# A mixture of experts in blocks of 128: rows turned between a block's two products, and blocks without tokens branched over

## The chip, the cores and the metric

The kernel runs on one core of a Trainium2 chip. A core has five engines with queues of their own: TensorE (PE in the profile; its weight loads are listed as PEld), VectorE (DVE), ScalarE (ACT), GpSimd (POOL) and SyncE (SP). They run beside each other and wait for each other by semaphores; transfers are done by DMA engines that SP, ACT and POOL ask. The metric is the device time of one execution in microseconds, and of several runs the median.

## The reference

Two layers. Attention between tokens and a state gives, for each of 8 batches, 512 token rows and 32 state rows of 512 values. Then each row goes to one of 8 experts:

```
logits = np.einsum('bsd,de->bse', x, w_gate)
local_gate = 1.0 / (1.0 + np.exp(-np.einsum('bsd,de->bse', x, w_local).squeeze(-1)))
...
        fresh_e = int(np.argmax(logits[b, s]))
        if s == 0 or local_gate[b, s] < 0.5:
            e = fresh_e
        else:
            e = prev_e if prev_e >= 0 else fresh_e
...
        h = np.maximum(x[b, s] @ w1[e], 0.0)
        out[b, s] = p[e] * (h @ w2[e])
```

w1 of an expert is 512 x 1024 and w2 is 1024 x 512, all in float32. There are 8 x 544 = 4352 rows. Which expert a row gets is known only while the kernel runs. With the inputs that the reference sets up, its own arithmetic gives the eight experts 1568, 600, 544, 512, 544, 40, 0 and 544 rows. In blocks of 128 that is 13, 5, 5, 4, 5, 1, 0 and 5, or 38 blocks.

## The kernel before, in words

`attention` goes through the batches and writes a row per token to DRAM (`rows`): 512 values and 8 gate probabilities. `Routing.route` then finds each token's expert and gives the tokens slots sorted by expert, an expert's slots filled up to whole blocks of 128. However the tokens fall, 34 full blocks and 7 broken ones are enough, so there are always NBLK = 41 blocks; the kernel does all 41, whether or not a block holds a token. `route` leaves three tables in SBUF: `gidx` (which row a slot gathers; row 0 where the slot is empty), `sidx` (where its result goes; a place past the end where it is empty, which the scatter leaves out) and `bei` (the expert of each block).

`experts` does the blocks one after the other. Block k:

- `load(k)`: SP reads the block's expert from `bei` into a register and asks for the two weights, `a` (w1) and `c` (w2), 2 MB each. There are two buffers of each, so `a` of block k + 2 is asked for when the first product of block k is done, and `c` of block k + 2 when its second is done.
- `gather(k)`: POOL asks for the block's 128 rows (`xg`, three buffers).
- DVE picks each row's probability for the block's expert (`own`, `p`).
- PE transposes the 128 x 512 rows in four pieces into PSUM (L428), and DVE copies the result to `x_t` (L430).
- First product (L437): 32 calls, two PE instructions each, from `x_t` and `a`; ACT takes each half out of PSUM with a ReLU into `h` (L439).
- Second product (L442): 8 calls, two instructions each, from `h` and `c`.
- DVE multiplies by the probability (`y`, L444), and POOL scatters the rows to their places (L445).

The program is traced in this order; a scheduler then lays out each engine's queue and puts in the semaphores. Each engine takes its queue strictly in order. On PE the queue reads, block after block: transposes, first product, second product. The first product needs the copy that DVE makes of the transposes just ahead of it.

Of the kernel before, what the change touches and what calls it, by code (L numbers as in the profile page):

```python
# [8 lines left out]
F32 = mybir.dt.float32  # L9
# [8 lines left out]
P = 128  # L18
# [20 lines left out]
def kernel(  # L39
# [33 lines left out]
    bei = keep.tile([1, NBLK], I32, name="bei")  # L73
    wg = keep.tile([P, KT, E + 1], F32, name="wg")
    nc.sync.dma_start(out=wg, in_=wgl.rearrange("p (k e) -> p k e", k=KT))
    # Logits of token (column i of 128, batch b); the last column holds the 32 state tokens.
# [7 lines left out]
    route.route(lt, mx, gidx, sidx, ohb, bei)  # L84
    with ExitStack() as phase:
        experts(phase, tc, bank, w1, w2, ident, rows, gidx, sidx, ohb, bei, out)


def attention(ctx, tc, bank, xn, xt, st, stt, ident, wg, lt, mx, rows):
# [8 lines left out]
    # State, and its transpose, with the heads of a group on the diagonal of blocks.  # L98
# [16 lines left out]
    # The state's gate logits: those of a token are the same mean of them as its values.  # L115
# [24 lines left out]
        # Tokens over state: scores of tokens over (head, state).  # L140
# [28 lines left out]
    def turned(e1, e2):  # L169
        """Both transposed: (head, state) over tokens, and tokens over (head, state)."""  # L170
# [12 lines left out]
    def read(b, a_t, e_t, x_n):  # L183
        # What the state reads, transposed, for pairs of heads; only a head's own block counts.
# [51 lines left out]
    # A batch's softmaxes run beside the products of the batch before it.  # L236
# [11 lines left out]
class Routing:  # L248
    """Tokens' experts, and the tokens of the slots."""
# [31 lines left out]
    def route(self, lt, mx, gidx, sidx, ohb, bei):  # L281
# [3 lines left out]
        # A token's own choice, the first of the largest logits, as 1..8, or 0 where it takes the one before.  # L285
# [14 lines left out]
        # In the order of a batch's tokens: the last choice made.  # L300
# [20 lines left out]
        # A token's place among those of its expert.  # L321
# [15 lines left out]
        nc.vector.tensor_tensor_scan(end[:, 0], ones[:, :E], nblk, 0.0, Alu.mult, Alu.add)  # L337
        first = rt.tile([P, E, 1], F32, name="first")
# [24 lines left out]
        # The experts of the blocks.  # L363
# [12 lines left out]
        # The tokens (from 1; 0 for none) of the slots, by (place in block, block).  # L376
# [16 lines left out]
def experts(ctx, tc, bank, w1, w2, ident, rows, gidx, sidx, ohb, bei, out):  # L393
# [3 lines left out]
    hp = ctx.enter_context(tc.tile_pool(name="hp", bufs=2))  # L397

    def gather(k):
        xg = gp.tile([P, XW], F32, name="xg")  # L400
        nc.gpsimd.indirect_dma_start(out=xg, out_offset=None, in_=rows[:, :],  # L401
                                     in_offset=bass.IndirectOffsetOnAxis(ap=gidx[:, k:k + 1], axis=0))
        return xg

    def load(k):
        e = nc.values_load(bei[0:1, k:k + 1], engines=[ET.SP], min_val=0, max_val=E - 1,
                           skip_runtime_bounds_check_because="the index of an expert")
        a = wp.tile([P, KT, F], F32, name="a")
        nc.sync.dma_start(out=a.rearrange("p k f -> p (k f)"),
                          in_=w1[bass.ds(e, 1)].rearrange("o p x -> (o p) x"))  # L410
        c = wp.tile([P, FK, D], F32, name="c")
# [65 lines left out]
```

## Time and profile before

| | us |
|---|---|
| median of 3 runs (lowest to highest) | 876.18 (876.18 to 879.81) |
| span of the profiled execution | 877.5 |
| first product of block 0 starts | 222.60 |
| y of block 40 starts | 867.91 |
| PE busy | 795.2 |

The page gives no time of the profiled execution beside its span, which is 1.3 us above the median of the runs. Up to about 200 us the core does attention and then finds the experts; the rest is the 41 blocks. In rows of the timeline stand the start, the duration, the engine, the line and operation, out<-in, the count, and in brackets how long the engine stood still before it and who ended that. Matmuls are pipelined, so a group's duration includes the last one's way through the array, and the next group starts before it ends. "L428" is a line of the kernel printed above.

### The profile page before, as it was taken

The page shows a single profiled execution, that of the slowest core. Times are in us where ns is not written, and L with a number is a line of the kernel's source. Part 1 is how long each engine was busy: PE and PEld are TensorE (multiplying, and loading weights), DVE is VectorE, ACT ScalarE, POOL GpSimd, SP SyncE. Part 2 cuts the span into 40 slices and gives each one's busy share as a digit, 9 for nine tenths or more (in the row PEclk, how much of TensorE's full clock was granted, in tenths as well). Part 3 has the DMA queues.
Part 4 walks back from the last instruction along what each step waited for, and adds up shares of the span by engine and source line. Part 5 has one row for each costly group of instructions (what it writes and reads, how often), then busy time and mean ns, then how long its engine had stood idle before and what let it go on. Part 6 is the DMA issues. An engine that isn't in the chain of part 4 may idle for free.

```text
span 877.5 us, 11051 instructions
## 1 busy us (share of the span) xinstructions
PE 795.2 (91%) x4658; PEld 600.2 (68%) x4658; DVE 182.8 (21%) x525; ACT 111.1 (13%) x200; POOL 103.5 (12%) x110
## 2 busy tenths in 40 slices
PE   6899999937899999999999999999999999999995
PEld 6588888927676666766757667576676766767663
DVE  2465555465100101001010010100101001001010
ACT  0333343310000010000100001000010000100000
POOL 2001110000110101101011010110100101001000
PEclk9799999965899999999999999999999999999998
DMA  8145531228488878888788788887888877788730
GB/s 335 49 148 177 198 118 55 102 87 354 155 318 301 297 286 304 321 297 300 277 306 317 292 296 292 307 316 281 297 298 303 316 287 290 292 307 308 271 144 1
DMA packets 25761, 219.41 MB, mean 250 GB/s; under 512 B 3760, under 2 KB 3760, under 8 KB 13168
## 3 DMA queue, kind: packets, MB, share of 16 engines
q1 hardware_dynamic: 14400, 189.29, 58.6%
q0 software_dynamic: 6560, 19.84, 6.0%
q10 hardware_dynamic: 4752, 9.58, 3.0%
q8 instruction: 37, 0.61, 0.3%
q14 instruction: 12, 0.10, 0.0%
HBM read 200.73 MB, written 19.80 MB: 251 GB/s over the span
## 4 chain that ended last, share of the span: by engine, by line
issue 65%; PE 21%; POOL 6%; DMA 4%; DVE 3%; POOLq 0%; SPq 0%; DVEq 0%
POOL out_dram L445 4%; PE ps L138 4%; PE ps L201 3%; PE ps L144 3%; PE ps L188 3%; DMA out_dram<-y,sidx 3%; PE ps L386 2%; POOL xg L401 2%; PE ps L121 2%; PE ps L204 1%; PE ps L178 1%; PE ps L173 1%; DMA sttc<-in_stt_dram 1%; DMA xg<-rows,gidx 0%; PE ps L214 0%
## 5 line engine op out<-in xcount | busy, mean ns | idle before, releaser
L437 PE MATMUL ps<-x_t,a 128*128 128x128 f32 x2624 | 305.9, 278 | 41.0 <-DVE x_t L430 41.0
L437 PEld LDWEIGHTS ps<-x_t,a 128*128 128x128 f32 x2624 | 298.1, 193 | 50.9 <-DVE x_t L430 50.9
L442 PE MATMUL ps<-c,h 128*128 128x512 f32 x656 | 288.3, 592 | 0.0
L442 PEld LDWEIGHTS ps<-c,h 128*128 128x128 f32 x656 | 121.5, 190 | 137.3 <-issue 137.3
L439 ACT ACTIVATE h<-ps 128x512 f32<-128x512 f32 x82 | 49.0, 597 | 632.5 <-PE ps L437 632.5
L401 POOL DMA_INDIRECT xg<-rows,gidx x41 | 40.0, 975 | 553.9 <-PE ps L428 500.0
L444 DVE TENSOR_SCALAR y<-ps,p 128x512 f32<-128x512 f32 x41 | 30.8, 751 | 284.6 <-PE ps L442 284.6
L423 DVE TENSOR_TENSOR own<-xg,ohb 128x8 f32<-128x8 f32 x41 | 6.9, 167 | 300.8 <-DMA xg<-rows,gidx 300.8
L445 POOL DMA_INDIRECT out_dram<-y,sidx x41 | 41.6, 1015 | 69.3 <-DVE y L444 58.0
L144 PEld LDWEIGHTS ps<-std,x_t 128*128 128x128 f32 x256 | 32.2, 197 | 8.8 <-issue 8.8
L428 PEld LDWEIGHTS ps<-ident,xg 128*128 128x128 f32 x164 | 20.7, 143 | 25.5 <-issue 25.5
L201 PE MATMUL ps<-sd,a 128*128 128x256 f32 x128 | 35.3, 398 | 0.0
L138 PE MATMUL ps<-x_t,std 128*128 128x512 f32 x64 | 33.7, 653 | 0.0
L166 POOL TENSOR_TENSOR e<-e,z 128x512 f32<-128x512 f32 x16 | 16.7, 1047 | 142.6 <-DVE z L160 109.6
L144 PE MATMUL ps<-std,x_t 128*128 128x128 f32 x256 | 32.0, 279 | 0.0
L188 PE MATMUL ps<-e,x_n 128*128 128x64 f32 x256 | 29.5, 273 | 0.0
L188 PEld LDWEIGHTS ps<-e,x_n 128*128 128x128 f32 x256 | 29.2, 192 | 0.0
L428 PE MATMUL ps<-ident,xg 128*128 128x128 f32 x164 | 25.1, 276 | 4.3 <-DMA xg<-rows,gidx 4.3
L430 DVE COPY x_t<-ps 128x512 f32<-128x512 f32 x41 | 27.9, 682 | 0.9 <-PE ps L428 0.9
L386 PE MATMUL ps<-bc,pc 128*128 128x41 f32 x80 | 17.3, 415 | 9.9 <-DVE bc L381 9.9
L386 PEld LDWEIGHTS ps<-bc,pc 128*128 128x128 f32 x80 | 17.1, 332 | 10.8 <-issue 10.8
L207 ACT COPY xr<-ps 128x512 f32<-128x512 f32 x32 | 18.8, 586 | 36.6 <-PE ps L201 36.6
(124 smaller groups left out, 343.1 us busy)
## 6 DMA issues: line engine op xcount, KB each, us to landing
a<-in_w_dram SPq DMA_DIRECT2D x41, 2048.0 KB, 7.8
c<-in_w_dram SPq DMA_DIRECT2D x41, 2048.0 KB, 8.9
rows<-xr ACTq DMA_DIRECT2D x8, 1040.0 KB, 4.3
x_t<-in_xt_dram SPq DMA_DIRECT2D x8, 1024.0 KB, 4.8
x_n<-in_xn_dram SPq DMA_DIRECT2D x8, 1024.0 KB, 5.4
xg<-rows,gidx POOLq DMA_INDIRECT x41, 8.4
out_dram<-y,sidx POOLq DMA_INDIRECT x41, 7.6
rows<-xs ACTq DMA_DIRECT2D x8, 65.0 KB, 4.0
```

Of the source, the lines that this page charges most:

```text
L138: nc.tensor.matmul(s2, lhsT=std[:, b, k, :], rhs=x_t[:, k, :], start=(k == 2 * g), stop=(k == 2 * g + 1))
L144: nc.tensor.matmul(s1[:, c * P:c * P + P], lhsT=x_t[:, k, c * P:c * P + P], rhs=std[:, b, k, :], start=(k == 2 * g), stop=(k == 2 * g + 1))
L188: nc.tensor.matmul(rps[:, k, :], lhsT=x_n[:, c, 2 * k:2 * k + 2, :].rearrange("p h d -> p (h d)"), rhs=e_t[k // 2][:, c, 64 * (k % 2):64 * ...
L201: nc.tensor.matmul(v[:, g * GD:g * GD + GD], lhsT=a_t[g][:, c * P:c * P + P], rhs=sd[:, b, g, :], start=True, stop=True)
L386: nc.tensor.matmul(who, lhsT=pc, rhs=bc[:, c], start=(c == 0), stop=(c == COLS - 1))
L401: nc.gpsimd.indirect_dma_start(out=xg, out_offset=None, in_=rows[:, :], in_offset=bass.IndirectOffsetOnAxis(ap=gidx[:, k:k + 1], axis=0))
L428: nc.tensor.transpose(tps[:, j * P:j * P + P], xg[:, j * P:j * P + P], ident)
L437: nc.tensor.matmul(hps[:, i * P:i * P + P], lhsT=a[:, j, m * P:m * P + P], rhs=x_t[:, j, :], start=(j == 0), stop=(j == KT - 1))
L439: nc.scalar.activation(h[:, half * 4:half * 4 + 4, :].rearrange("p m t -> p (m t)"), hps, Act.Relu)
L442: nc.tensor.matmul(yps, lhsT=h[:, m, :], rhs=c[:, m, :], start=(m == 0), stop=(m == FK - 1))
L444: nc.vector.tensor_scalar(y, yps, p, None, Alu.mult)
L445: nc.gpsimd.indirect_dma_start(out=out, out_offset=bass.IndirectOffsetOnAxis(ap=sidx[:, k:k + 1], axis=0), in_=y, in_offset=None, bounds_c ...
```

## The change

The transposes, the copy to `x_t` and the probabilities of block k become a function `turn(k)`. It is called once ahead of the first block, and then within block k for block k + 1, between the two products, together with the loads of block k + 1's weights. The buffers of `experts` are now tiles by hand, numbered by k modulo 2, and modulo 4 for `xg`, so gathers are asked for one block further ahead. `route` writes the number of blocks with tokens to `nbi`, one more small cast on DVE. Every engine reads `nbi` into a register. Blocks 0 to 33 are done always; blocks 34 to 40 stand each within an `If` of the one before, and where the number of blocks is reached, all that is left is jumped over. What is skipped would have written nothing, as such a block's slots are all empty. Comments are dropped as well.

```diff
+        nc.vector.tensor_copy(nbi, end[0:1, 0, E - 1:E])
...
-    wp = ctx.enter_context(tc.tile_pool(name="wp", bufs=2))
-    gp = ctx.enter_context(tc.tile_pool(name="gp", bufs=3))
+
+    fx = ctx.enter_context(tc.tile_pool(name="fx", bufs=1))
     hp = ctx.enter_context(tc.tile_pool(name="hp", bufs=2))
+    as_ = [fx.tile([P, KT, F], F32, name=f"a{i}") for i in range(2)]
+    cs_ = [fx.tile([P, FK, D], F32, name=f"c{i}") for i in range(2)]
+    xgs_ = [fx.tile([P, XW], F32, name=f"xg{i}") for i in range(4)]
+    xts_ = [fx.tile([P, KT, P], F32, name=f"x_t{i}") for i in range(2)]
...
-    xgs = {k: gather(k) for k in range(2)}
-    for k in range(NBLK):
-        a, c = load(k)
-        if k + 2 < NBLK:
-            xgs[k + 2] = gather(k + 2)
-        xg = xgs.pop(k)
-        own = gp.tile([P, E], F32, name="own")
-        nc.vector.tensor_tensor(own, xg[:, D:], ohb[:, k], op=Alu.mult)
-        p = gp.tile([P, 1], F32, name="p")
-        nc.vector.tensor_reduce(p, own, axis=AX, op=Alu.add)
+    def turn(k, xg):
+
         tps = bank()
         for j in range(KT):
             nc.tensor.transpose(tps[:, j * P:j * P + P], xg[:, j * P:j * P + P], ident)
-        x_t = hp.tile([P, KT, P], F32, name="x_t")
+        x_t, own, p = xts_[k % 2], owns_[k % 2], ps_[k % 2]
         nc.vector.tensor_copy(x_t.rearrange("p k t -> p (k t)"), tps)
+        nc.vector.tensor_tensor(own, xg[:, D:], ohb[:, k], op=Alu.mult)
+        nc.vector.tensor_reduce(p, own, axis=AX, op=Alu.add)
+        return x_t, p
+
+    xgs = {k: gather(k) for k in range(3)}
+    ws = {0: load(0)}
+    ready = {0: turn(0, xgs.pop(0))}
+
+    def block(k):
+        a, c = ws.pop(k)
+        x_t, p = ready.pop(k)
         h = hp.tile([P, FK, P], F32, name="h")
...
+        if k + 1 < NBLK:
+            ws[k + 1] = load(k + 1)
+            ready[k + 1] = turn(k + 1, xgs.pop(k + 1))
+        if k + 3 < NBLK:
+            xgs[k + 3] = gather(k + 3)
         yps = bank()
...
+    n = nc.values_load(nbi[0:1, 0:1], min_val=NJ, max_val=NBLK,
+                       skip_runtime_bounds_check_because="a number of blocks")
+    for k in range(NJ):
+        block(k)
+    with ExitStack() as held:
+        for k in range(NJ, NBLK):
+            held.enter_context(tc.If(n > k))
+            block(k)
```

What this makes of the queues is shown at three places. A wait in brackets names what the instruction waits for: DMAHW the weights, DMASW a gather or scatter, else an engine. First PE, one block in the middle of the stage, before (L428 transposes, L437 first product, L442 second product):

```order
L428 MATMUL ps<-ident,xg 128x128 [waits DMASW2_49,PE_49]
L428 MATMUL ps<-ident,xg 128x128 x3
L437 MATMUL ps<-x_t,a 128x128 [waits DMAHW1_49,DVE_49]
L437 MATMUL ps<-x_t,a 128x128 x15
L437 MATMUL ps<-x_t,a 128x128 [waits PE_49]
L442 MATMUL ps<-c,h 128x512 [waits DMAHW2_49,Activation_49]
L442 MATMUL ps<-c,h 128x512 x3
L442 MATMUL ps<-c,h 128x512 [waits Activation_49]
```

and the same block now (L447 first product, L427 transposes, L458 second product):

```order
L447 MATMUL ps<-x_t_1736,a_1728 128x128 [waits DMAHW1_49,DVE_49]
L447 MATMUL ps<-x_t_1736,a_1728 128x128 x15
L447 MATMUL ps<-x_t_1736,a_1728 128x128 [waits PE_49]
L427 MATMUL ps<-ident,xg_1731 128x128 [waits DMASW3_49,PE_49]
L427 MATMUL ps<-ident,xg_1731 128x128 x3
L458 MATMUL ps<-c_1730,h 128x512 [waits DMAHW2_49,Activation_49]
L458 MATMUL ps<-c_1730,h 128x512 x3
L458 MATMUL ps<-c_1730,h 128x512 [waits Activation_49]
```

The transposes, now the next block's, have moved from ahead of the first product to between the two; the first product's wait for DVE is for a copy that has the whole second product ahead of it in PE's queue.

Then DVE, the same part of the stage, before (L430 the copy to x_t, L444 y, L423 and L425 the probabilities):

```order
L430 COPY x_t<-ps 128x512 [waits PE_49]
L425 TENSOR_REDUCE p<-own 128x1 [waits DVE_49]
L423 TENSOR_TENSOR own<-xg,ohb 128x8 [waits DMASW0_49]
L444 TENSOR_SCALAR y<-ps,p 128x512 [waits DMASW7_49,PE_49]
L430 COPY x_t<-ps 128x512 [waits PE_49]
```

and now (L429 the copy, L460 y, L430 and L431 the probabilities):

```order
L431 TENSOR_REDUCE p_1739<-own_1737 128x1 [waits DVE_49]
L430 TENSOR_TENSOR own_1737<-xg_1733,ohb 128x8 [waits DMASW7_49,DVE_49]
L429 COPY x_t_1735<-ps 128x512 [waits PE_49]
L460 TENSOR_SCALAR y<-ps,p_1740 128x512 [waits DMASW0_49,PE_49]
L431 TENSOR_REDUCE p_1740<-own_1738 128x1 [waits DVE_49]
```

The copy, which came behind the y of the block before, now comes ahead of it, and it has `own` ahead of it, which waits for a gather.

Last PE where block 33 ends and block 34 begins; before, the queue goes on there as in the first piece:

```order
L458 MATMUL ps<-c_1730,h 128x512 [waits Activation_49]
L458 MATMUL ps<-c_1730,h 128x512 x3
L465 TENSOR_LOAD nbi [waits DVE_49]
L469 COMPARE_AND_BRANCH
L447 MATMUL ps<-x_t_1735,a_1727 128x128 [waits DMAHW7_49,DVE_49,PE_49]
L447 MATMUL ps<-x_t_1735,a_1727 128x128 x15
```

The number of blocks is read into a register here, not earlier, and a comparison with a branch stands ahead of the block; one such branch stands ahead of each of the blocks 35 to 40 too, and the other four engines have the same rows in their queues.

More of the change, by code (lines that the diff above doesn't have):

```diff
@@ L83 @@
         attention(phase, tc, bank, xn, xt, st, stt, ident, wg, lt, mx, rows)
-    route.route(lt, mx, gidx, sidx, ohb, bei)
+    route.route(lt, mx, gidx, sidx, ohb, bei, nbi)
     with ExitStack() as phase:
-        experts(phase, tc, bank, w1, w2, ident, rows, gidx, sidx, ohb, bei, out)
+        experts(phase, tc, bank, w1, w2, ident, rows, gidx, sidx, ohb, bei, nbi, out)
 def attention(ctx, tc, bank, xn, xt, st, stt, ident, wg, lt, mx, rows):
@@ L279, in __init__, with route @@
         self.consts = iof, tok1, far, before, ones, ev, down, full, on
-    def route(self, lt, mx, gidx, sidx, ohb, bei):
+    def route(self, lt, mx, gidx, sidx, ohb, bei, nbi):
         nc, rt, bank, ident = self.nc, self.rt, self.bank, self.ident
```

10 lines of the change are left out of this document (6 added, 4 removed).

## The prediction

> **What bounds the kernel now.** I read three views in this order: the page's busy times and chain, the list of waits, then the timeline of one block. Names: P1 is a block's first product, P2 its second, T the four transposes of a block's rows, the copy is the move of T's result from PSUM to x_t, y is the scaled result.
>
> ```profile
> PE 795.2 (91%) x4658; PEld 600.2 (68%) x4658; DVE 182.8 (21%) x525; ACT 111.1 (13%) x200; POOL 103.5 (12%) x110
> issue 65%; PE 21%; POOL 6%; DMA 4%; DVE 3%; POOLq 0%; SPq 0%; DVEq 0%
> PE ps L437 <- DVE x_t L430: 41.0, 41, 1.0
> ```
>
> PE is the busy engine. The chain of waits puts 65% on "issue", that is, it cannot follow the expert stage and tells nothing there. The last row does: PE's wait in a block is for the copy, 1.0 us each time, 41 times.
>
> ```profile
> core 0: us, PE busy (x) PEld busy (x) DVE busy (x) ACT busy (x) POOL busy (x), PEclk, DMA share, GB/s
> 50.00:186.00 136.00, 130.55 (x950) 113.19 (x949) 73.20 (x238) 49.66 (x98) 13.61 (x13) 0.99 0.38 135
> 222.00:227.00 5.00, 4.40 (x20) 4.40 (x21) 1.28 (x6) 0.00 (x0) 0.94 (x1) 0.50 0.30 94
> 271.84:743.60 471.76, 441.60 (x2521) 318.21 (x2521) 47.53 (x121) 35.83 (x60) 59.79 (x61) 1.00 0.82 300
> 806.00:822.00 16.00, 14.72 (x84) 10.60 (x84) 1.86 (x5) 1.19 (x2) 1.91 (x3) 1.00 0.86 304
> 838.00:854.00 16.00, 14.99 (x87) 10.88 (x88) 1.35 (x2) 1.19 (x2) 1.26 (x2) 1.00 0.29 118
> 854.00:870.00 16.00, 13.87 (x79) 9.69 (x77) 0.75 (x1) 1.20 (x2) 1.18 (x2) 1.00 0.01 1
> ```
>
> The row of 30 blocks has PE busy 441.6 of 471.76 us at clock 1.00, and the DMA engines at 0.82. The last two rows tell two things. The weights have stopped by then (share 0.29, then 0.01), and, as the times below show, blocks 39 and 40 are no shorter for it: DMA is not what paces a block. And 854 to 870 moves 1 GB/s, some 16 KB, where a scatter of 128 full rows is 262 KB: block 39's scatter writes nothing, which fits the count of 38 blocks with tokens out of the reference's choices. Blocks 38, 39 and 40 compute for nobody.
>
> Here is block 1 to block 2, and the end:
>
> ```profile
> 240.40 7.41 PE L437 MATMUL ps<-x_t,a 128*128 128x128 f32 x64 [1.00 <-DVE x_t L430]
> 247.65 7.03 PE L442 MATMUL ps<-c,h 128*128 128x512 f32 x16
> 254.51 0.60 PE L428 MATMUL ps<-ident,xg 128*128 128x128 f32 x4
> 255.38 0.68 DVE L430 COPY x_t<-ps 128x512 f32<-128x512 f32 x1
> 256.12 7.41 PE L437 MATMUL ps<-x_t,a 128*128 128x128 f32 x64 [1.01 <-DVE x_t L430]
> ...
> 853.59 7.41 PE L437 MATMUL ps<-x_t,a 128*128 128x128 f32 x64 [1.01 <-DVE x_t L430]
> 860.84 7.03 PE L442 MATMUL ps<-c,h 128*128 128x512 f32 x16
> 867.91 0.75 DVE L444 TENSOR_SCALAR y<-ps,p 128x512 f32<-128x512 f32 x1 [14.37 <-PE ps L442]
> 868.94 0.98 POOL L445 DMA_INDIRECT out_dram<-y,sidx  x1 [14.74 <-DVE y L444]
> ```
>
> Starts count, since ends overlap. P1 takes 7.25 us of the block (240.40 to 247.65), P2 6.86 (to 254.51), T with the wait 1.61 (to 256.12): a block is 15.72, and (853.59 - 240.40) / 39 = 15.723 says that all 39 are so.
>
> **The change part by part.**
>
> *T moved between P1 and P2.* The wait goes only if P2 covers the copy. T ends, the copy follows 0.27 us later and takes 0.68, so x_t is there about 1 us into P2's 6.86. On DVE the copy of block k+1 now has own of block k+3 ahead of it, which waits for a gather; those rows are asked for after the scatter of block k-3, about two blocks earlier, and land within 10.6 us at the worst:
>
> ```profile
> a<-in_w_dram SPq DMA_DIRECT2D x41, 2048.0 KB, 7.8
> c<-in_w_dram SPq DMA_DIRECT2D x41, 2048.0 KB, 8.9
> DMA to landing us min/median/max: 3.6/8.4/10.6
> ```
>
> (the last row is the gather's). P2 does not wait longer for the second half of h than now: T only comes between. What T, P1 and P2 cost when nothing stops PE is read from pitches:
>
> ```profile
> 241.28 5.97 PE L437 MATMUL ps<-x_t,a 128*128 128x128 f32 x52
> 57.25 0.66 PE L173 MATMUL ps<-ident,e 128*128 128x128 f32 x4
> 57.75 0.60 PE L178 MATMUL ps<-ident,e 128*128 128x128 f32 x4
> 58.18 0.60 PE L173 MATMUL ps<-ident,e 128*128 128x128 f32 x4
> ```
>
> 52 instructions of P1 last 5.97 us; less the last one's own 0.274 that is 5.70 / 51 = 0.1117 each, 64 of them 7.15. The 0.10 up to 7.25 is the restart after the wait. Four transposes in an unbroken row take 0.43 (57.75 to 58.18) to 0.50 (57.25 to 57.75). So the new block is 7.15 + 6.86 + 0.47 = 14.48. Bounds: 7.15 + 6.86 + 0.43 = 14.44 below, and 7.25 + 6.86 + 0.60 = 14.71 above, if P1 keeps its restart and T counts with its whole record. I take 14.48, since attention shows such changes of shape without a gap.
>
> *The first block.* PE runs it half at clock 0.50 (row 222 to 227 above); that stays.
>
> ```profile
> 222.60 9.48 PE L437 MATMUL ps<-x_t,a 128*128 128x128 f32 x64 [0.78 <-DVE x_t L430]
> 231.92 7.03 PE L442 MATMUL ps<-c,h 128*128 128x512 f32 x16
> ```
>
> P2 of block 0 starts at 231.92; with T ahead of it, block 1 starts at 231.92 + 0.47 + 6.86 = 239.25 instead of 240.40.
>
> *Three blocks fewer.* Blocks 1 to 37 are 37 x 14.48 = 535.8, so P2 of block 37 ends at 775.0 and its y starts 0.2 later (y of block 40 starts 0.21 after 853.59 + 7.25 + 6.86 = 867.70): 775.2 instead of 867.9, 92.7 less. Of that the three blocks are 3 x 15.72 = 47.2 and the rest, 45.5, is the wait with the restart. Block 37 still loads weights and turns rows for block 38; both lie in the 14.48 and the free DMA time.
>
> *What the branches add.* The page has no branch and no register load as rows. Nearest is SP, which reads a block's expert into a register between two issues, and the cast that is added sits beside a scan of eight values:
>
> ```profile
> 190.54 0.17 DVE L337 TENSOR_TENSOR_SCAN end<-ones,nblk 128x8 f32<-128x8 f32 x1
> 194.36 0.34 SPq L412 DMA_DIRECT2D c<-in_w_dram  x1
> 195.21 0.33 SPq L409 DMA_DIRECT2D a<-in_w_dram  x1
> ```
>
> 195.21 - 194.70 = 0.51 for the load and what the address needs. PE has one register load and four branches into blocks 34 to 37. Lower bound 0: PE's sequencer may do them while P2's last matmuls, 0.43 each, are still running. Upper bound 5 x 0.51 = 2.6, if each stops PE for as long as SP needed. I take 1.0, nearer the lower end, since the load's own wait is for a value written 600 us earlier. [...] The cast adds 0.17 to DVE's row of work before the gathers. SP, ACT, DVE and POOL branch too. Behind them queue the next weights, h, the copy and the gathers, each wanted several us later or, for the weights, 14 us: a is asked for when P1 of block k ends, lands after 7.8 and is used 0.47 + 6.86 + 14.48 = 21.8 later.
>
> *The end.* From y's start to the span's end are 877.5 - 867.9 = 9.6 us.
>
> ```profile
> L473 POOLq DRAIN  x3: 40/107/7987, 868.7 to 877.2; - x3
> L473 PEldq DRAIN  x2: 13/3112/6212, 861.7 to 877.0; - x2
> L473 SPq DRAIN  x3: 7/7/7, 871.3 to 877.0; - x3
> ```
>
> POOL's drain of 7.99 us fills nearly all of it; SP had its last landing by 871.3. The last scatter now writes 32 rows instead of none, and lands, by the gather's 3.6 with little else running, at most 1.5 later than 871.3: hidden beside the drain. Each engine's one jump over blocks 38 to 40 comes at the end too. [...]
>
> The sum: -92.7 + 0.17 + 1.0 + 0.5 = -91.0, so the span goes from 877.5 to 786.5. The profiled execution stands 1.3 above the median of the runs, 876.18; against the median it is **785**. Own range: 14.44 a block and no costs give 782; 14.71 (+8.5), branches at 2.6 (+1.6) and a bare jump (+3.1) give 798. So 781 to 798.
>
> **The rivals.**
>
> *Entering a block costs a fetch.* If the branch into a block, and not only the jump past them, makes an engine ask memory for its instructions, PE stands still at each. Price by the shortest round trip here, 3.6: four entries and the last jump are 18, less the 1.5 counted: 785 + 16.5 = 801. For it speaks that nothing in this trace excludes it; against it, the blocks follow each other in the order of the program, so that nothing new is asked for. [...]
>
> *The weights become the bound.* A block moves 4.19 MB of weights and 0.53 of rows; 0.82 x 15.72 = 12.9 us of DMA time. If 0.86, the highest share of a block here, is all that can be had, a block is 12.9 / 0.86 = 15.0 and the time 785 + 37 x 0.52 = 804. Against it: each load waits for its buffer, and each block has stretches without any transfer, as this half microsecond (PE, clock, DMA share, GB/s):
>
> ```profile
> 248.00:248.50 0.50, 0.50 (x2) 1.00 0.00 0
> ```
>
> *The change does not do what it says.* Either no block is skipped (three more at 14.48: 828) or PE waits elsewhere for 1.24 a block (37 x 1.24 = 46: 831). The order of instructions and the row 854 to 870 speak against both.
>
> *Slower.* One mechanism: PE is now busy without a pause and its granted clock falls for the whole stage. Below 535.8 / (535.8 + 91) = 0.855 the kernel is slower than before; at 0.80 it would be 785 + 134 = 919. For it: the clock does move here (0.50 in the row 222 to 227). Against it: that was after idleness, and 130.55 of 136 us busy in attention kept 0.99.
>
> **How the numbers follow.** Forecast 0.77; fetch at each entry 0.11; weights 0.07; change without one of its effects 0.03; slower 0.02. What the two likeliest rivals would give is 801 and 804, and some of each lies below, so the range is 779 to 803. A measurement here can't tell 0.5%, about 4 us, from no change; all but the slower case lie far past it: faster 0.97, same 0.01, slower 0.02.
>
> **What would show it.** Right: P1 starts 14.4 to 14.6 apart from block 1 to 33; no PE wait for the copy; the gap before P1 of blocks 34 to 37 under 1 us; 38 pairs of products; from y of block 37 to the end about 10 us. Wrong: a gap of 3 to 4 us before each of those four blocks (fetch); PE waiting for a or c (weights); a clock under 1.00 after 240 us; an end well over 13 us, which would be the jump.

## The result, and the profile after

| | us |
|---|---|
| median before, beside these runs (4 runs) | 877.4 (876.18 to 879.81) |
| median of the changed kernel (4 runs) | 784.18 (783.41 to 785.57) |
| ratio, 95% interval | 0.893, 0.891 to 0.895 |
| span of the profiled execution, and its time | 783.0, and 784.79 |
| span predicted, and time predicted | 786.5, and 785 |

The kernel is 93.2 us faster, 0.8 us from the forecast. The same three views, of the changed kernel: the page's busy times and chain, the wait list (PE's row, which now stands for one wait instead of 41) and the window of the middle of the stage.

```profile
PE 739.7 (94%) x4410; PEld 568.0 (73%) x4410; DVE 185.4 (24%) x517; ACT 107.5 (14%) x194; POOL 100.6 (13%) x107
PE 92%; DVE 3%; DMA 2%; issue 1%; POOL 0%; SPq 0%; POOLq 0%; DVEq 0%
```

```profile
PE ps L447 <- DVE x_t L429: 0.8, 1, 0.8
```

```profile
271.84:700.00 428.16, 428.16 (x2476) 313.55 (x2475) 51.86 (x116) 35.23 (x59) 57.70 (x58) 1.00 0.88 326
```

PE is busy for 428.16 of 428.16 us at clock 1.00. The DMA engines' share rose from 0.82 to 0.88: the same bytes a block in less time, and no wait for them. And the chain can be read now: before, 65% of it was "issue" and nothing could be followed through the expert stage; a chain of 92% PE is what it looks like when one engine has no pauses. That one wait of 0.8 is block 0's.

The timeline at the place of the change (P1 L447, T L427, the copy L429, P2 L458, y L460, scatter L461; columns as before), and the starts of the first product through the branched blocks to the end:

```profile
700.18 7.31 PE L447 MATMUL ps<-x_t,a 128*128 128x128 f32 x64
707.33 0.60 PE L427 MATMUL ps<-ident,xg 128*128 128x128 f32 x4
707.76 4.46 PE L458 MATMUL ps<-c,h 128*128 128x512 f32 x10
707.96 0.69 DVE L429 COPY x_t<-ps 128x512 f32<-128x512 f32 x1 [6.63 <-PE ps L427]
...
714.63 7.31 PE L447 MATMUL ps<-x_t,a 128*128 128x128 f32 x64
729.08 7.31 PE L447 MATMUL ps<-x_t,a 128*128 128x128 f32 x64
757.98 7.31 PE L447 MATMUL ps<-x_t,a 128*128 128x128 f32 x64
772.63 0.75 DVE L460 TENSOR_SCALAR y<-ps,p 128x512 f32<-128x512 f32 x1 [6.18 <-PE ps L458]
```

P1 takes 7.15 (700.18 to 707.33), T 0.43 (to 707.76), P2 6.87 (to 714.63): a block is 14.45, and the blocks behind a branch (714.63, 729.08, and two on 757.98) are no longer. The copy is done at 708.65, 5.98 us before P1 wants it, so its cover was never in doubt.

The first two blocks in the timeline, and then the branches and drains with their own times (minimum, median and maximum in ns, first and last start in us):

```profile
221.23 9.41 PE L447 MATMUL ps<-x_t,a 128*128 128x128 f32 x64 [0.78 <-DVE x_t L429]
237.78 7.31 PE L447 MATMUL ps<-x_t,a 128*128 128x128 f32 x64
```

```profile
L465 PEldq TENSOR_LOAD <-nbi x1: 484/484/484, 708.2 to 708.2; - x1
L469 PEldq COMPARE_BRANCH  x6: 65/78/3382, 708.8 to 772.8; - x6
L469 POOLq INC_SWDGE_SEM  x1: 1769/1769/1769, 773.7 to 773.7; - x1
L499 POOLq DRAIN  x3: 46/107/6512, 775.7 to 782.7; - x3
L499 PEldq DRAIN  x2: 8/8/8, 773.0 to 782.5; - x2
```

PE's queue reads the number of blocks at 708.2, while the array is at the start of block 33's second product; the first matmul behind the branch starts at 714.63. The queue is 6.4 us ahead there, so neither the load (0.48) nor an entered branch (0.07 to 0.09) stops the array. The branch over blocks 38 to 40 is taken and lasts 3.38 us, from 766.0 on, while block 37's second product keeps the array busy to 772.6. The sixth row is one of 0.20 us at 772.8, behind the last product.

### The profile page after: what moved, and what is told of

Its sections match the earlier page's. It is cut to its first block, busy times and chain, and to the rows that moved or that the text cites. A ratio compares the mean times of both kernels' runs of the same rounds, so it can differ in the third digit from the quotient of the medians.

```text
span 783.0 us, 10576 instructions
## 1 busy us (share of the span) xinstructions
PE 739.7 (94%) x4410; PEld 568.0 (73%) x4410; DVE 185.4 (24%) x517; ACT 107.5 (14%) x194; POOL 100.6 (13%) x107
## 4 chain that ended last, share of the span: by engine, by line
PE 92%; DVE 3%; DMA 2%; issue 1%; POOL 0%; SPq 0%; POOLq 0%; DVEq 0%
PE ps L447 34%; PE ps L458 32%; PE ps L139 4%; PE ps L202 4%; PE ps L145 4%; PE ps L189 4%; PE ps L388 2%; PE ps L427 2%; PE ps L122 2%; PE ps L205 1%; DMA out_dram<-y,sidx 1%; PE ps L179 1%; PE ps L174 1%; DMA sttc<-in_stt_dram 1%; PE ps L215 0%
## 5 line engine op out<-in xcount | busy, mean ns | idle before, releaser
L447 PEld LDWEIGHTS ps<-x_t,a 128*128 128x128 f32 x2432 | 279.5, 193 | 18.9 <-issue 17.7
L447 PE MATMUL ps<-x_t,a 128*128 128x128 f32 x2432 | 279.8, 276 | 0.8 <-DVE x_t L429 0.8
L458 PE MATMUL ps<-c,h 128*128 128x512 f32 x608 | 267.2, 592 | 0.0
L458 PEld LDWEIGHTS ps<-c,h 128*128 128x128 f32 x608 | 112.6, 190 | 127.2 <-issue 127.2
L449 ACT ACTIVATE h<-ps 128x512 f32<-128x512 f32 x76 | 45.4, 597 | 541.6 <-PE ps L447 541.6
L429 DVE COPY x_t<-ps 128x512 f32<-128x512 f32 x39 | 27.0, 692 | 246.6 <-PE ps L427 246.6
L460 DVE TENSOR_SCALAR y<-ps,p 128x512 f32<-128x512 f32 x38 | 28.5, 751 | 234.8 <-PE ps L458 234.8
L461 POOL DMA_INDIRECT out_dram<-y,sidx x38 | 38.4, 1011 | 289.5 <-DVE p L431 263.9
L189 PE MATMUL ps<-e,x_n 128*128 128x64 f32 x256 | 29.5, 273 | 0.0
L189 PEld LDWEIGHTS ps<-e,x_n 128*128 128x128 f32 x256 | 29.2, 192 | 0.0
L427 PE MATMUL ps<-ident,xg 128*128 128x128 f32 x156 | 23.9, 277 | 4.1 <-DMA xg<-rows,gidx 4.1
L388 PE MATMUL ps<-bc,pc 128*128 128x41 f32 x80 | 17.3, 415 | 9.9 <-DVE bc L383 9.9
L202 PEld LDWEIGHTS ps<-sd,a 128*128 128x128 f32 x128 | 21.9, 191 | 1.6
L427 PEld LDWEIGHTS ps<-ident,xg 128*128 128x128 f32 x156 | 18.6, 143 | 4.3 <-issue 4.3
```

Source lines behind the costliest of these rows:

```text
L189: nc.tensor.matmul(rps[:, k, :], lhsT=x_n[:, c, 2 * k:2 * k + 2, :].rearrange("p h d -> p (h d)"), rhs=e_t[k // 2][:, c, 64 * (k % 2):64 * ...
L202: nc.tensor.matmul(v[:, g * GD:g * GD + GD], lhsT=a_t[g][:, c * P:c * P + P], rhs=sd[:, b, g, :], start=True, stop=True)
L388: nc.tensor.matmul(who, lhsT=pc, rhs=bc[:, c], start=(c == 0), stop=(c == COLS - 1))
L427: nc.tensor.transpose(tps[:, j * P:j * P + P], xg[:, j * P:j * P + P], ident)
L447: nc.tensor.matmul(hps[:, i * P:i * P + P], lhsT=a[:, j, m * P:m * P + P], rhs=x_t[:, j, :], start=(j == 0), stop=(j == KT - 1))
L449: nc.scalar.activation(h[:, half * 4:half * 4 + 4, :].rearrange("p m t -> p (m t)"), hps, Act.Relu)
```

## Experiments

Each is the changed kernel with the edit shown, beside runs of the kernel before on the same chip, whose median was between 877.7 and 878.3. In each, the stretch from P1 of block 1 to y of block 37 is a good measure: it has no part of the start or the end in it. In the changed kernel it is 772.63 - 237.78 = 534.85.

### 1. The transposes moved, no block skipped

```diff
-    n = nc.values_load(nbi[0:1, 0:1], min_val=NJ, max_val=NBLK,
-                       skip_runtime_bounds_check_because="a number of blocks")
-    for k in range(NJ):
-        block(k)
-    with ExitStack() as held:
-        for k in range(NJ, NBLK):
-            held.enter_context(tc.If(n > k))
-            block(k)
+    for k in range(NBLK):
+        block(k)
```

> The transposes moved, all 41 blocks done, no branch and no register load of the number of blocks. My theory: each block of the changed kernel is 14.45 us, so three more of them are 43.4, and the span is 783.0 + 43.4 = 826.4, or 825.6 if the end is 0.8 shorter without the branches. P1 starts 14.45 apart. Rival, the branches themselves cost something in the changed kernel (0.5 us for each of five): the span is below 824. Rival, the wait went because of the branches or the hand-made buffers and not because of the move: a block is 15.72 again and the span is near 877.

Measured: 826.98 us, ratio 0.9415 (0.9389 to 0.9441), so about 51 us less than before. P1 of block 1 starts at 237.74 and y of block 40 at 815.50: 577.76, which is 40 blocks of 14.45, less the last one's T (0.43), plus the 0.2 from P2's end to y. The stall with its restart was worth 40 x 1.27 = 51, the part that the prediction gave as 45.5 for the 37 blocks that are left (1.23 each).

### 2. Blocks branched over, the transposes where they were

```diff
...
     def block(k):
-        a, c = ws.pop(k)
-        x_t, p = ready.pop(k)
+        a, c = load(k)
+        if k + 2 < NBLK:
+            xgs[k + 2] = gather(k + 2)
+        x_t, p = turn(k, xgs.pop(k))
...
-        if k + 1 < NBLK:
-            ws[k + 1] = load(k + 1)
-            ready[k + 1] = turn(k + 1, xgs.pop(k + 1))
-        if k + 3 < NBLK:
-            xgs[k + 3] = gather(k + 3)
```

> The branches and the hand-made buffers, but each block's transposes are ahead of its own first product as before. My theory: 15.72 a block, 38 of them; the span is 877.5 - 3 x 15.72 = 830.3, with the later start of the end 0.8 more, with a start of the stage like that of the changed kernel 1.4 less: 829 to 831.5. Entering blocks 34 to 37 adds nothing, since PE's queue is asked long before the array gets there. Rival, a branch costs PE 0.5 or more where PE stands still at the head of a block anyway: 833 or more, seen as longer gaps ahead of blocks 34 to 37.

Measured: 833.38 us, ratio 0.9487 (0.9457 to 0.9516). From P1 of block 1 to y of block 37 (239.42 to 820.92) it is 581.50, 1.15 over 36 x 15.723 + 7.25 + 6.86 + 0.21 = 580.35 (L453 is P2 here, L455 y). The hand-made buffers are in this run too, and its unbranched blocks still take 15.72, so the buffers are not what shortens a block. A block without a branch, and one behind a branch:

```profile
630.89 0.60 PE L427 MATMUL ps<-ident,xg 128*128 128x128 f32 x4
631.09 0.75 DVE L455 TENSOR_SCALAR y<-ps,p 128x512 f32<-128x512 f32 x1 [14.11 <-PE ps L453]
631.76 0.68 DVE L429 COPY x_t<-ps 128x512 f32<-128x512 f32 x1
...
772.74 0.60 PE L427 MATMUL ps<-ident,xg 128*128 128x128 f32 x4
772.94 0.75 DVE L455 TENSOR_SCALAR y<-ps,p 128x512 f32<-128x512 f32 x1 [14.38 <-PE ps L453]
773.61 0.16 DVE L430 TENSOR_TENSOR own<-xg,ohb 128x8 f32<-128x8 f32 x1
773.80 0.16 DVE L431 TENSOR_REDUCE p<-own 128x1 f32<-128x8 f32 x1
773.88 0.68 DVE L429 COPY x_t<-ps 128x512 f32<-128x512 f32 x1
774.62 7.41 PE L447 MATMUL ps<-x_t,a 128*128 128x128 f32 x64 [1.27 <-DVE x_t L429]
```

The excess of 0.3 a block is no branch instruction. Within a branched block the scheduler didn't reach back over the branch, so `own` and its sum, 0.27 us, stand between y and the copy, and the copy is on the path in this order. With the transposes moved the copy has 5.98 us to spare, so the changed kernel pays nothing there. Alone, the two parts give about 51 and 44 us; together 93, since the stall is then saved on three blocks fewer.

### 3. The transposes late in the second product

```diff
-            ready[k + 1] = turn(k + 1, xgs.pop(k + 1))
+            pass
...
         for m in range(FK):
+            if m == FK - 1 and k + 1 < NBLK:
+                ready[k + 1] = turn(k + 1, xgs.pop(k + 1))
             nc.tensor.matmul(yps, lhsT=h[:, m, :], rhs=c[:, m, :], start=(m == 0), stop=(m == FK - 1))
```

> The changed kernel, but the next block's transposes stand ahead of the last of P2's eight calls, so that only one call, 2 x 0.43 = 0.86 us, covers the copy. My theory (what P2 hides is the 1.17 us from the transposes' end in the array to the copy's end, with 0.10 for the restart): a wait of 1.17 - 0.86 = 0.31 and the restart, 0.41 a block, 14.86 a block, span 783.0 + 37 x 0.41 = 798. Rival, the move pays by something else (fewer changes of shape, other buffers): the span stays at 783. Rival, the copy is late for another reason than PE's own time (own waits for a gather): more than 0.5 a block, above 801.

Measured: 791.89 us, ratio 0.9011 (0.8984 to 0.9038): the cover of only one call of P2, 2 x 0.43 = 0.86 us, costs 0.19 a block (14.64 from one P1 to the next) and not the 0.41 expected. T, P2's last call, and the next P1 (L460 is P2, L462 y here):

```profile
499.91 0.60 PE L427 MATMUL ps<-ident,xg 128*128 128x128 f32 x4
500.35 1.02 PE L460 MATMUL ps<-c,h 128*128 128x512 f32 x2
500.55 0.69 DVE L429 COPY x_t<-ps 128x512 f32<-128x512 f32 x1 [12.63 <-PE ps L427]
501.29 7.41 PE L447 MATMUL ps<-x_t,a 128*128 128x128 f32 x64
501.41 0.75 DVE L462 TENSOR_SCALAR y<-ps,p 128x512 f32<-128x512 f32 x1 [0.17 <-PE ps L460]
```

From T's start to P1 there are 1.38 us, where the kernel before took 1.61. Here the copy starts 0.64 after T's start, there 0.87 (255.38 - 254.51, in the rows of the prediction), because there DVE first had the y of the block before, in the kernel before's own timeline:

```profile
254.72 0.75 DVE L444 TENSOR_SCALAR y<-ps,p 128x512 f32<-128x512 f32 x1 [6.49 <-PE ps L442]
```

The copy follows 0.66 later, at 255.38. So of the stall of before, 0.23 a block was y standing ahead of the copy, which the prediction didn't see; it read the copy's wait as T and the copy alone. Moving T behind P1 took that away too, so the forecast of the block didn't suffer by it.

### 4. A branch ahead of every block

```diff
...
-    for k in range(NJ):
+    for k in range(1):
         block(k)
     with ExitStack() as held:
-        for k in range(NJ, NBLK):
+        for k in range(1, NBLK):
```

> The changed kernel, but each of the blocks 1 to 40 stands within a branch on the number of blocks; 37 are entered instead of 4. My theory: the comparison runs in the queue while the array still works off the product before, so nothing is added, 783 to 785. Rival, entering costs what the register load costs, 0.5: 33 x 0.5 = 16, near 800. Rival, each entry makes an engine fetch (3.4 as the one jump of PE shows): 33 x 3.4 = 112, near 895.

Measured: 788.85 us, ratio 0.8968 (0.8935 to 0.9).

```profile
L469 PEldq COMPARE_BRANCH  x39: 65/65/3501, 234.5 to 775.4; - x39
```

From P1 of block 1 (240.38) to y of block 37 (775.24) it is 534.86 us, with 33 more branches entered than in the changed kernel's 534.85: an entered branch costs nothing measurable. The first of them is reached at 234.5, 5.9 us before its block starts. What the run is slower by lies outside: attention's first product with the softmax (L189) starts at 48.65 instead of 46.37, which is told below, and the end, from y on, is 12.96 us instead of 10.37. POOL's drain begins 2.7 us after its last semaphore write instead of 0.2. POOL's last branch stands between the two, and its own row is 0.05 us; that it has more code to jump past here is a guess that was not tested.

### 5 and 6. What a taken branch costs, with and without work ahead of it

To see jumps in the middle of the stage, a body of 128 matmuls that is never entered was put into blocks 3, 7, ... 31, eight in all:

```diff
+    def never(k):
+        with tc.If(n > 60):
+            d = bank()
+            for i in range(128):
+                nc.tensor.matmul(d[:, :P], lhsT=ident, rhs=ident, start=True, stop=True)
```

In run 5 it stands in the changed order, and ends up behind the first call of the second product; in run 6 in the order of experiment 2, behind the first call of the first product, where PE has just waited for the copy.

> The changed kernel with eight bodies of 128 small matmuls that are never entered, one each in blocks 3, 7, ... 31, behind the first call of P2. PE jumps over each. My theory: the jump takes PE's queue about 3.4 us, as at the end of the changed kernel, and hides, since the queue gets there while the array has part of P1, T and one call of P2 before it, some 4 us: span 783 to 787. Rival, a jump stops the array for its whole length: 8 x 3.4 = 27, near 810.

> The order of before with branches, as in the run with the branches alone, and the same eight bodies that are never entered, but behind the first call of P1, which waits for the copy, so that the queue gets to the jump with one call of 0.22 us left in the array. My theory: the jump stands open, 3.4 less 0.2, so 3.2 each: 8 x 3.2 = 26 above the run with the branches alone, 855 to 858. Rival, jumps over what is not entered cost next to nothing in mid-stream and the 3.4 us at the end belong to the end of the program: the same as that run, 829 to 832.

Measured: 807.71 us (ratio 0.919, 0.9147 to 0.9233) and 906.24 us (1.0319, 1.03 to 1.0339). The first is 23.5 over the changed kernel, 2.9 a jump, where the theory had next to nothing; the second is 73 over experiment 2, 9.1 a jump where 3.2 was expected, and slower than the kernel before. Of run 5 the eight branches on PE, and the timeline at the first:

```profile
L469 PEldq COMPARE_BRANCH  x8: 3501/4510/5298, 275.2 to 700.8; - x8
```

```profile
276.33 1.02 PE L458 MATMUL ps<-c,h 128*128 128x512 f32 x2
279.23 6.25 PE L458 MATMUL ps<-c,h 128*128 128x512 f32 x14 [1.88 <-PEq L469]
```

And of run 6 the same (L456 is P1 there), with the window of the first jump behind:

```profile
L440 PEldq COMPARE_BRANCH  x8: 5787/6184/6541, 273.2 to 775.5; - x8
```

```profile
272.60 0.49 PE L456 MATMUL ps<-x_t,a 128*128 128x128 f32 x2 [1.00 <-DVE x_t L429]
279.37 0.98 PE L456 MATMUL ps<-x_t,a 128*128 128x128 f32 x3 [6.29 <-PEq L440]
282.19 8.59 PE L456 MATMUL ps<-x_t,a 128*128 128x128 f32 x59 [1.84 <-issue]
```

```profile
273.00:279.00 6.00, 0.09 (x1) 0.00 (x0) 0.07 (x1) 0.00 (x0) 1.01 (x1) 0.72 0.90 354
```

Three things are to be seen. The jump itself takes 3.5 to 6.5 us here, against 3.38 at the end of the changed kernel: here the weights have the DMA engines (share 0.90), there they had little to do (0.15 between 766.0 and 769.4). That this is what lengthens it isn't shown; at a like share run 5 has 3.5 to 5.3 and run 6 has 5.8 to 6.5. At the first jump of run 6, and at none of its others, three matmuls pass behind the landing and then comes a second pause without a wait, 1.84 us. And after the wait the clock is down (0.78 in P1 behind the first jump of run 6): 59 matmuls take 8.59 us, where the last 59 of the next block's P1 take 6.75, and behind the last jump 62 matmuls take 9.75. So of the 9.1 a jump some 6 are the wait (47.6 in all eight), and most of the rest is slower matmuls. What PE's queue does during a jump is not shown. The row of the instruction queue has 53 packets (0.87 MB) in experiment 7 below, where eight such jumps are taken too, against 37 (0.61 MB) in experiment 4, the same kernel without them, two more for each jump, though some of them may be the bodies' own code. Only PE has matmuls to jump over, and only PE pays: the other four engines' rows of these branches are 0.04 to 0.07 us. How long a jump must be to cost this was not tried.

Why was run 5 not covered, where PE is never short of work? The queue came to the branch at 275.2, and the two matmuls of P2 that stand ahead of it last from 276.33 to 277.35: a lead of 2 us. What the array still had to do at 275.2 were, at 0.11 each, some six matmuls of P1, four of T and these two, twelve in all, and most of them short. At a block's end the 15 matmuls that stand ahead are all P2's, 0.43 each, 6.4 us. From these two the lead looks like a number of instructions, some 12 to 15 matmuls with their weight loads, and not a time, which is an estimate. If so, the same jump at a block's head is covered. That is the next run.

### 7. The same jumps at the head of a block

```diff
...
         for k in range(1, NBLK):
             held.enter_context(tc.If(n > k))
+            if k < NJ and k % 4 == 3:
+                never()
             block(k)
```

on the kernel of experiment 4.

> The kernel with an If ahead of every block, and eight never-entered bodies of 128 matmuls as in the two runs before, but now at the head of blocks 3, 7, ... 31, where 16 calls of the second product stand ahead of the branch in PE's queue. Theory (PE's queue runs ahead by a number of instructions, some 15 matmuls; there these last 15 x 0.43 = 6.4 us): a jump of 4.5 to 6.2 us is covered or nearly so, 0 to 1 us each over the 788 of the kernel with an If ahead of every block, so 786 to 796, and rows of PE waiting for its own queue under 1 us or none. Rival A (the lead is 2 us wherever the branch stands): some 3 us each, 812. Rival B (a jump costs its whole fetch and what follows it, wherever it stands): 6 to 9 us each, 836 to 860.

Measured: 800.81 us, ratio 0.9124 (0.9102 to 0.9145), 12 over experiment 4, or 1.5 a jump. From P1 of block 1 to y of block 37 (236.37 to 783.52) it is 547.15, 12.3 over 534.85. The eight jumps, and then in the timeline the first of them and a later one:

```profile
L468 PEldq COMPARE_BRANCH  x8: 6445/6574/7196, 259.0 to 674.6; - x8
```

```profile
266.06 0.57 PE L447 MATMUL ps<-x_t,a 128*128 128x128 f32 x3 [0.63 <-PEq L468]
269.83 9.34 PE L447 MATMUL ps<-x_t,a 128*128 128x128 f32 x61 [3.21 <-issue]
...
388.70 7.38 PE L447 MATMUL ps<-x_t,a 128*128 128x128 f32 x64 [0.50 <-PEq L468]
```

Each jump takes 6.4 to 7.2 us. Ahead of P1 the array waits 0.3 to 0.6 behind seven of them, and 1.04 behind the longest, at 557.0, where the wait is put down to DVE's `own`; the other 6 are covered, by 15 matmuls of 0.43. Of the 12.3 us more than half, 6.6, is the first jump alone (P1 of block 4 starts 35.50 after P1 of block 2, not 28.90), with its second pause of 3.21 and the slower matmuls behind it; the other seven cost 0.8 each in the mean, two of them 1.2 and 1.3. So the lead is not 2 us wherever the branch stands; a number of matmuls, 12 there and 15 here, fits both, though not exactly. The total misses the 786 to 796 that was expected: the jumps were longer than the 4.5 to 6.2 supposed, and the first one, as in run 6, has a second pause. The last jump has one as well, of 0.43 us; where these pauses come from stays open.

### 8. No branch and no register at all

```diff
-    n = nc.values_load(nbi[0:1, 0:1], min_val=NJ, max_val=NBLK,
-                       skip_runtime_bounds_check_because="a number of blocks")
-    for k in range(NJ):
-        block(k)
-    with ExitStack() as held:
-        for k in range(NJ, NBLK):
-            held.enter_context(tc.If(n > k))
-            block(k)
+    for k in range(38):
+        block(k)
```

> The changed order without any branch or register for the number of blocks: the loop simply does 38 blocks, which is right for these inputs alone. Theory (entries of blocks and the jump on PE are hidden): from the first product of block 1 to y of block 37 534.8 to 534.9 us, as in the changed kernel, and a time within 2 us of its 784.2. For the end: if the 0.8 us more than before from y to the end come of the 32 rows that the last scatter writes, they stay here (10.3 to 10.4); if they come of the branches, the end is 9.6 again. Rival (the branches cost the 1.0 that was predicted, somewhere that was not looked at): 533.8 or less between the two, and 781 to 782.

Measured: 783.03 us, ratio 0.892 (0.8898 to 0.8942). P1 of block 1 is at 236.24 and y of block 37 at 771.09; POOL's drains stand behind the timeline:

```profile
236.24 7.31 PE L447 MATMUL ps<-x_t,a 128*128 128x128 f32 x64
771.09 0.75 DVE L460 TENSOR_SCALAR y<-ps,p 128x512 f32<-128x512 f32 x1 [6.18 <-PE ps L458]
```

```profile
L493 POOLq DRAIN  x3: 40/107/7745, 771.9 to 780.2; - x3
```

Between the two there are again 534.85 us, with no branch in them. The end is 780.4 - 771.09 = 9.3 us, against 10.4 with branches (10.37 in the changed kernel, 10.3 in experiment 2) and 9.6 without (the kernel before and experiment 1). The last scatter writes its 32 rows here as well, so they are not what lengthens the end: it is POOL's part of the branching. In the changed kernel POOL writes a semaphore (INC_SWDGE_SEM), 1.77 us from 773.7, and only then drains; this run has no such row. That leaves about 1 us as the whole price of the branches in this kernel.

### 9 to 11. The start: a clock that falls

The changed kernel's stage began 1.4 us sooner than predicted, and its runs, like those of before, differ by 2 to 4 us. The trace shows the granted clock at 0.72 between 33 and 45 us, and at 0.50 through the routing until the first block. So products that are needed for nothing were put where PE waits for DVE: `warm(4)`, `warm(4)`, `warm(15)` and `warm(7, pc)` at four places of the routing (run 9); these, three calls of 128x512 ahead of attention's first block and one product of 128 columns beside every third of the 41-column ones (run 10); and run 9's with the three calls in attention alone (run 11).

```diff
+        def warm(calls, by=ident):
+            d = bank()
+            for i in range(calls):
+                nc.tensor.matmul(d[:, :E * COLS], lhsT=by, rhs=on.rearrange("p e c -> p (e c)"), start=True, stop=True)
```

> The changed kernel with needless matmuls of 320 columns between and behind those of the routing (4, 4, 15 and 7 calls), so that PE has no long pause between attention and the first block. What is to be seen is whether the half clock of that stretch (0.50 from 186 to 222 us) comes from the pauses and what it costs. Theory, it comes from pauses: with clock 1.00, P1 of block 0 takes 7.2 instead of 9.3 and the 40 small products of the routing, at 0.43 each, are then paced by VectorE's 0.29: 2 + 5 less, and the span is 776 to 779. Rival, the clock there has another cause: the clock stays at 0.50, the needless work runs at half speed, the 15 calls take 16 us where 10 are free, and the span is 788 to 792.

> The run with needless products in the routing, with more of them: three calls of 128x512 ahead of the attention's first block, and one 128-column product beside every third 41-column product. Theory (the clock falls where the columns that pass per microsecond are few, not only where PE idles): the clock stays at 1.00 from 180 us on through the 41-column products, these take about 12 to 14 us instead of 15.7, and the time is 777 to 781 (from attention's start to the first product of block 1 some 184 us instead of 187.6). Rival (the fall has another cause, or the added products cost what they bring): clock 0.50 again at 203 to 215, and 783 or more.

> The needless products of the first such run (four places in the routing) and the three calls of 128x512 ahead of the attention's first block, without the ones beside the 41-column products, which cost more than they brought. Theory (each place acts for itself: three calls keep the clock at 1.00 from 33 to 45 us, so that the attention's product starts at 44.0 instead of 46.4 to 48.7; the four places in the routing make it 187.6 us from there to the first product of block 1 instead of 191.4): P1 of block 1 at 231.6, the span 231.6 + 534.85 + 10.4 = 777, the time 778 to 780. Rival (where the clock opens in the attention is chance, and the calls had no part in it): start 45 to 49 as in the other runs, and a time of 782 to 785.

Measured: 782.6 us (ratio 0.8913, 0.89 to 0.8927), 786.89 (0.896, 0.8942 to 0.8978) and 780.78 (0.8894, 0.8879 to 0.8909). All three miss their forecasts, run 11 by 0.8 us. Attention's product with the softmax (first start behind the durations) in the changed kernel, then in runs 10 and 11:

```profile
L189 PE MATMUL ps<-e,x_n x256: 222/275/275, 46.4 to 171.7; 128*128 128x64 f32 x128
```

```profile
L189 PE MATMUL ps<-e,x_n x256: 222/275/275, 44.0 to 169.3; 128*128 128x64 f32 x128
```

```profile
L189 PE MATMUL ps<-e,x_n x256: 222/275/275, 44.3 to 169.7; 128*128 128x64 f32 x128
```

The window from 33 to 45 us before, then in the changed kernel, and for run 11 two windows and the timeline:

```profile
33.00:45.00 12.00, 10.30 (x38) 6.98 (x39) 5.01 (x14) 2.10 (x5) 2.09 (x2) 0.60 0.11 48
```

```profile
33.00:45.00 12.00, 9.87 (x40) 6.43 (x41) 5.54 (x14) 2.43 (x5) 1.84 (x2) 0.72 0.07 29
```

```profile
33.00:45.00 12.00, 9.39 (x61) 7.11 (x59) 7.73 (x19) 3.36 (x7) 2.36 (x3) 1.00 0.24 88
199.00:203.00 4.00, 4.00 (x21) 4.00 (x20) 2.74 (x10) 0.00 (x0) 0.00 (x0) 0.50 0.99 426
```

```profile
195.04 17.06 PE L399 MATMUL ps<-bc,pc 128*128 128x41 f32 x80 [2.37 <-DVE bc L394]
219.04 7.41 PE L459 MATMUL ps<-x_t,a 128*128 128x128 f32 x64 [0.79 <-DVE x_t L441]
```

In the runs without the three calls this start lies anywhere between 44.8 (experiment 8) and 48.65, and it goes with the clock in that window: 48.2 to 48.65 at 0.57, 47.6 at 0.60, 46.1 to 46.7 at 0.72, 44.8 and 45.0 at 1.00. With the calls it is 44.0 and 44.3 at 1.00. But the two runs that reach 1.00 without them (experiments 7 and 8) were made on the same chip as run 10, and against these the calls of run 10 bring 0.9 to 1.0 us. That the calls set the clock is not shown: the rival of chance stands, and a difference between chips beside it. Nor is the scatter of the times shown to come from there. The five times of run 11 lie within 0.65 us, against 2.2 us in the changed kernel; but those of run 10, with the calls, spread over 1.47, and those of run 9 and experiment 1, without them, over 0.76 and 0.72. Why the start moves by 3.9 us between the runs without the calls stays open.

In the routing the needless products bring block 0 to full clock, 7.41 us instead of 9.41. Around the start of the 41-column products, though, the clock goes from 1.00 to 0.50 in all three, and stays there with PE busy the whole time; the denser work of run 10 didn't lift it, made these products longer (194.66 to 217.26, 22.6 us instead of 17.3) and cost more than it brought. That theory fell. Just ahead of the products PE still stands still for 2.4 us, waiting for DVE's `bc`, and in run 10 the clock is at 0.50 from 194.6 on, before the first of them at 194.66: the pause may be what lets it fall, which no run shows. What keeps it down after that, beside weights that come in at 426 GB/s at that time, stays open. The same edits of the routing brought 3.8 us in run 9 and 2.2 in run 11 (from attention's product to P1 of block 1 191.41 in the changed kernel, 187.61 and 189.25), which is why run 11 came out later than expected. It is the best version found all the same: 3.4 us under the changed kernel, 0.4%, at five small edits.

## Why the prediction was right, point by point

In spans the forecast was 3.5 us too long (786.5 against 783.0); in times, 0.8.

- **What bounds the kernel.** Right: PE, with the wait for the copy as its only regular pause. It read that wait as T and the copy; 0.23 of the 1.61 was y ahead of the copy on DVE (experiment 3). The step says only that the wait goes if P2 covers the copy, and it does, with 6 us to spare.
- **The block.** Right: 14.45 for 14.48. The term taken as 0.47 for T was 0.43, the lower bound of the two rows in attention. Over 37 blocks, 1.1 us.
- **Three blocks fewer.** Right: 38 pairs of products, and 3 x 14.45 = 43.4 between experiment 1 and the changed kernel. From P1 of block 1 to the last y it is 577.76 - 534.85 = 42.9, since experiment 1's last block has no T.
- **The start.** Mis-sized by 1.64 us: P1 of block 1 was at 237.78, predicted 239.25 and 0.17 for the cast. 1.37 of it was there at block 0 (221.23 for 222.60), and attention's product already started 1.3 sooner (46.37 for 47.64). That lies ahead of anything that the change touches, and goes with the clock from 33 to 45 us, 0.72 for 0.60; why the clock differs there from run to run stays open. What stands beside it, that block 0 runs half at clock 0.50, was right.
- **The branches, 1.0.** Entering costs 0 (534.85 with four, 534.86 with 37, 534.85 with none). The lower bound was the true one, and for the reason given: the queue does them while P2's last matmuls run. The value was taken too near the middle, though the argument for zero stood there. PE's four entered branches took 65 to 92 ns each, and none of it is on the path.
- **The end, 9.6 and 0.5.** It is 10.37, 0.3 more than that. No run shows the 0.5 that the sum takes for the jump, nor the 3.1 more that the range takes for a bare one. What the runs show is PE's jump of 3.38 us, covered by P2 of the last block (6.87 us), rows of POOL's branches of 0.03 to 0.05 us, and POOL's semaphore write of 1.77 us ahead of a drain that is 1.5 us shorter (6.51 for 7.99); without branches the end is 9.3 (experiment 8). With the entries, the whole allowance for branches and end was 1.5, and some 1 was used.
- **From span to time.** The prediction took 1.3 off, because the span stood 1.3 above the median. But in each run of the changed kernel the time is 1.8 to 2.3 above its span, so the profiled run of before had a time of some 879.3 or more, an estimate, at the top of its range and 3.1 above the median, not 1.3; that of the changed kernel was only 0.6 above its own. The sum of the terms was 3.5 too long, and this took 2.5 of it back: -3.5 + 2.5 = -1.0 from the 785.2 worked out. Part of the closeness is luck.
- **The rivals.** Fetch at each entry: no, 0.07 to 0.09 us and hidden; but a taken jump took 5.8 to 6.5 us where little stood ahead of it (experiment 6), against the 3.6 at which the rival priced an entry. Weights: share 0.88 without a wait. The supposed ceiling, 0.86, was no ceiling. Change without one of its effects, and the falling clock: no, 38 blocks at 14.45 and 1.00.

The terms add up: -1.64 (start) - 1.1 (blocks) - 1.0 (entries) + 0.27 (end) = -3.5.

## What to carry to other kernels

The stall of the busy engine for another's short step, a copy of 0.68 us, was worth its whole length here, restart and all, 1.27 us of a block's 15.72, once the step had one other product of 6.87 us for cover; look on the other engine for what stands ahead of that step, since that belonged to the stall too (0.23). A branch that is entered cost this kernel nothing where PE's queue was some 6 us ahead, as long as no step on the path had to stay behind it (experiment 2). A jump of PE's over three blocks or 128 matmuls took 3.4 to 7.2 us here, and only the instructions still queued ahead of it hid that, all of it behind 15 matmuls of 0.43 us at the end, all but 0.3 to 1.04 at a block's head, some 0.2 of 6.2 in run 6: put it behind the longest ones. Take a sum of terms against the time that belongs to the same execution, and look at the start of the program before ascribing a few us to a change that comes after it.

## What was not expected of the hardware

- PE's queue came to a branch about 2 us ahead of the array where 12 matmuls, most of them short, stood ahead of it (run 5), and 5.9 to 6.4 us ahead where 15 of 0.43 us did (experiment 4 and the changed kernel). That the lead is a number of instructions is an estimate from these.
- A taken branch took PE 3.4 us at the end of the changed kernel, 3.5 to 6.5 within a block, up to 7.2 at a block's head; behind the first jump of two runs a second pause of 1.84 or 3.21 us follows, and the clock is down behind them, 0.78 in run 6 after a wait of 6.29 us and that pause, 0.73 in experiment 7.
- The clock stays at 0.50 while PE is busy without a pause, in products of 41 columns (12.00 of 12.00 us from 203 to 215 in run 9), and is at 1.00 again from 219 on, in products of 320 columns.
- Where blocks are branched over, POOL's end has a semaphore write, of 1.77 us in the changed kernel and in experiments 4 and 7 and of 1.75 in experiment 2; experiment 8, without branches, has none.
